# Earlier FFN weight and LayerNorm fetches, LayerNorms split from their transposes, weight loads on two queues and whole-row V copies in a memory-transformer kernel

## The chip, the cores and the metric

The kernel runs on one core of a Trainium2 chip. The metric is the device time of one execution in microseconds (us). Absolute times differ between chips: the kernel before took 1549 us (median) on the chip of the first comparison and 1564 to 1567 us on the chips of the three later calls. Kernels of different calls are compared by their ratio to the kernel before, which ran beside them on the same chip; kernels of one call also by their medians. A ratio is the mean time of one kernel's fast runs over the mean of the other's fast runs of the same rounds, so it is not quite the ratio of the medians quoted.

Stage boundaries are read from a profiled execution's timeline, in us from the start of the span. TensorE is called PE in the profile, VectorE DVE, ScalarE ACT, SyncE SP; SPq and ACTq are the instruction streams that issue DMAs.

## The reference, cut to what matters

```python
# x: 2048 x 640, bf16; 32 heads of 128; 8 memory rows; segments of 32 tokens
mem = mem0
for s in range(64):
    h = concat([mem, ln1(x)[32*s : 32*s+32]])        # 40 rows
    q, k, v = h @ Wq, h @ Wk, h @ Wv                 # 640 -> 32*128 each
    p = softmax(mask(q @ k.T * 128**-0.5))
    o = (p @ v) @ Wo                                 # 32*128 -> 640
    mem = o[:8]                                      # feeds the next segment
    attn[32*s : 32*s+32] = o[8:]
h  = x + attn
h2 = h + (relu(ln2(h) @ W_gate) * (ln2(h) @ W_up)) @ W_down      # 640 -> 1728 -> 640
```

The 64 segments form a chain through `mem`. The FFN at the end has no chain; it runs in 4 blocks of 512 rows.

## The kernel before

Operations are recorded in program order for each engine. A small dependency solver turns read and write keys (`r=`, `w=`) into semaphore waits. Each engine works strictly in its own order, and so does the SP queue that issues nearly all DMAs: a DMA that must wait holds up every later one. All DMAs carry the line of the helper, L298, so tile names tell them apart.

Names used below: a pass is the product with one weight matrix (the K pass with Wk, the Wo pass with Wo); KmT and Vr hold keys and values, oT the attention's output on its way into the Wo pass, xt the rows that a LayerNorm works on, hT the product of gate and up. LN1 and LN2 are the two LayerNorms; "row i" of LN2 is a block of 128 rows. "Segments 1 mod 4" are segments 1, 5, 9 and so on.

The FFN's tensors lie in the SBUF space of the attention weights: Wg and Wu in that of Wq, Wd in that of Wk, the rest in that of Wk and Wv. The parts that matter:

```python
# LN1: one piece, in every fourth segment, in PE order before KmT is copied
def ln1(b, n, bk):
    norm_rows(xt, ("xt",), n, xt, ("xt",))     # DVE statistics, ACT Ln and Exp, DVE scale
    transpose_rows(xt, ("xt",), n, bk)         # five PE transposes (L314)
    ...                                        # DVE copies to the operands of the passes

# LN2: one piece too
def ln2(i, bk):
    par, u, e = (i // 4) % 2, i % 4, i % 2     # two buffers xt2, at
    dma(x2, x_ap[128*i:128*i+128, :], r=[("Wdone",)], w=[xk])
    dma(a2, attn_d[...], r=attn_keys(i) + [("Wdone",)], w=[ak])
    add("dve", ... h = x2 + a2 ...)
    norm_rows(h, hk, 128, x2, xk)
    transpose_rows(x2, xk, 128, bk)
    copy_op("act", xn2T[par][...], ...)

# V rows for later segments, 8 pieces of 256 bytes in each row
dma(Vr[q][..., 0:Dh], Vp[par][..., 0:Dh], ...)

# start: all loads on SP
ld_init = ln1_load(-1)
for j in (1, 0, 2):
    for i in range(2):
        dma(W[:, j, :, 2048*i:2048*i+2048], ..., w=[("W", j, i)])
dma(Wo[:, :, :], ..., w=[("Wo",)])
ln1(-1, ld_init, XP0)
ln1(0, ln1_load(0), XP1)                       # second x block: behind all weights
... 64 segments ...
# after the last segment
dma(Wg, ..., w=[("W", 0, 0), ("W", 0, 1), ("Wg",)])
dma(Wu, ..., w=[("W", 0, 0), ("W", 0, 1), ("Wu",)])
dma(Wd[:, 0:FC-1, :], ..., w=[("W", 1, 0), ..., ("Wd", 0)])
dma(Wd[0:FR, FC-1, :], ..., w=[("W", 1, 0), ..., ("Wd", 1)])
... last attention outputs and their stores, ln2(0) to ln2(3) ...
for b in range(NBLK):
    for j in range(FC):
        gate_up(b, j)
        if b + 1 < NBLK and j in (2, 4, 6, 8):
            ln2(4*(b+1) + (2, 4, 6, 8).index(j), BT[j // 2 % 2])
    for u in range(4):
        down(b, u)
```

Wg and Wu both write the key `("W", 0, 0)`. To the solver that is a write after a write, so Wu waits until Wg has landed although they fill different bytes. The same holds for the two pieces of Wd.

The softmax here doesn't subtract the row's maximum and nothing guards it: scores larger than these inputs give would overflow.

## Time and profile before

Median 1548.69 us of 3 runs (1544.54 to 1549.66). The page of the kernel before: TensorE's busy time, its busy tenths and its granted clock in 40 equal slices of the span, and the DMA packets.

```profile
PE 1275.4 (82%) x36507; PEld 809.4 (52%) x36507; DVE 632.3 (41%) x1687; ACT 415.6 (27%) x736; POOL 4.1 (0%) x21
...
PE   0289898989898988988898889898989825878698
...
PEclk9999999999999999999999999999999967989899
...
DMA packets 86829, 58.02 MB, mean 37 GB/s; under 512 B 67376, under 2 KB 81392, under 8 KB 86512
```

PE is near full in the long middle. The holes are at the start, in slice 33 (segments to FFN) and, shallower, in the FFN. Why the start is empty is in the timeline of the SP queue (start, duration, what was issued):

```profile
8.89 1.15 SPq L298 DMA_DIRECT2D W<-in_A_Wk_dram  x2
...
11.38 19.17 SPq L298 DMA_DIRECT2D W<-in_A_Wv_dram  x2
30.59 6.20 SPq L298 DMA_DIRECT2D Wo<-in_A_Wo_dram  x1
36.91 20.98 SPq L298 DMA_DIRECT2D xt<-in_A_x_dram  x1
```

The second x block (`xt`) is issued after 21 MB of weights; its own issue blocks for 21 us, it lands at 65.4, and the first K pass starts at 68.3. The SP queue's own waits around the transition (total us, times, longest):

```profile
SPq L298 <- DMA Wd<-in_B_W_down_dram: 14.3, 1, 14.3
...
SPq L298 <- DMA Wg<-in_B_W_gate_dram: 9.0, 1, 9.0
```

These two are the shared keys at work: SP stood on Wu until Wg had landed, and on Wd's small last piece until Wd's main piece had landed. The longest of PE's waits between the last segment and the FFN (1240 to 1292) is for the first LN2 rows, whose loads stand behind all this on SP:

```profile
PE ps L314 <- DVE xt_0_98 L308: 26.1, 2, 23.2
```

Then PE's waits in the FFN:

```profile
PE ps L314 <- DVE xt_0_98 L308: 20.8, 6, 3.5
PE ps L314 <- DVE xt_1_99 L308: 20.8, 6, 3.5
```

Twelve times PE reached LN2's transposes (L314) and waited 3.5 us for DVE, in all 41.6 us. PE's waits in segments 2 to 62:

```profile
PE ps L564 <- issue: 31.8, 30, 1.6
PE ps L514 <- issue: 25.1, 32, 1.9
PE ps L314 <- DVE xt L308: 12.2, 14, 0.9
```

The third line is the same thing for LN1. "issue" means that PE waited for nothing that the profile shows. Laid beside the DMA records, every such gap ends 1.2 to 1.5 us (5th to 95th percentile) after a 16 KB packet of the instruction queue has finished, so I read them as PE running out of instructions. Counting gaps over 0.3 us, they are 83.7 us of segments 2 to 62. (The view counts from 0.15 us, so its lines add up to 1 to 3 us more. "Segments 2 to 62" are, here and below, the 60 segments from the end of segment 1's Wo pass to the end of segment 61's.)

### The profile page before, as it was taken

The numbers are of one execution on the slowest core, as the hardware profiler recorded it, in microseconds if no ns is written. First come the engines' busy times: TensorE is split into PE (matmuls) and PEld (weight loads), VectorE is DVE, ScalarE is ACT, GpSimd is POOL, SyncE is SP. The second block draws the span as 40 slices with busy tenths as digits, with TensorE's granted clock in tenths as the row PEclk, the third lists the DMA queues.
The fourth block names the chain that finished last, engine by engine and source line by source line (L and its number), as shares of the span: only waits on it lengthen the run. The fifth ranks groups of instructions, "written<-read, shape, count | busy, mean of one in ns | idle before, by whom it ended". The sixth has DMA issues, their size and how long they took to land.

```text
span 1554.2 us, 77215 instructions
## 1 busy us (share of the span) xinstructions
PE 1275.4 (82%) x36507; PEld 809.4 (52%) x36507; DVE 632.3 (41%) x1687; ACT 415.6 (27%) x736; POOL 4.1 (0%) x21
## 2 busy tenths in 40 slices
PE   0289898989898988988898889898989825878698
PEld 0156555656556555655665555565556622434254
DVE  1144444444444445444444444444444413232322
ACT  0032233333232333322232323323323202121211
POOL 1000000000000000000000000000000000000000
PEclk9999999999999999999999999999999967989899
DMA  7601110101000000100000001110000151011000
GB/s 294 253 14 19 21 21 17 22 15 24 17 21 17 20 17 21 21 21 17 21 21 17 20 17 22 19 22 17 18 17 16 25 183 51 9 43 34 17 18 18
DMA packets 86829, 58.02 MB, mean 37 GB/s; under 512 B 67376, under 2 KB 81392, under 8 KB 86512
## 3 DMA queue, kind: packets, MB, share of 16 engines
q1 hardware_dynamic: 86512, 53.09, 12.3%
q8 instruction: 285, 4.67, 1.3%
q14 instruction: 32, 0.26, 0.1%
HBM read 35.48 MB, written 5.24 MB: 26 GB/s over the span
## 4 chain that ended last, share of the span: by engine, by line
PE 74%; DVE 9%; issue 7%; DMA 4%; ACT 3%; SPq 3%; POOL 0%; DVEq 0%; POOLq 0%
PE ps L330 23%; PE ps L514 12%; PE ps L350 10%; PE ps L776 9%; PE ps L564 5%; PE ps L798 4%; PE ps L364 4%; SPq L298 3%; DVE tok_73 L337 2%; DMA xt<-in_A_x_dram 2%; DVE st L302 2%; PE ps L535 1%; PE ps L532 1%; PE ps L490 1%; PE ps L314 1%
## 5 line engine op out<-in xcount | busy, mean ns | idle before, releaser
L330 PE MATMUL ps<-W,act_r_67 128*32 128x512 bf16 x2680 | 154.9, 383 | 2.7 <-DVE rx L575 1.4
L330 PE MATMUL ps<-W,act_r_66 128*32 128x512 bf16 x2560 | 148.9, 384 | 2.4 <-issue 2.3
L335 ACT ACTIVATE tok_70<-ps 128x512 bf16<-128x512 f32 x65 | 38.8, 597 | 354.6 <-PE ps L330 354.6
L330 PEld LDWEIGHTS ps<-W,act_r_67 128*32 128x32 bf16 x2680 | 69.8, 97 | 74.2 <-DVE tok_71 L337 6.6
L514 PE MATMUL ps<-Wo,oT_88 128*32 128x160 bf16 x4224 | 88.2, 239 | 21.4 <-issue 16.1
L330 PEld LDWEIGHTS ps<-W,act_r_66 128*32 128x32 bf16 x2560 | 67.7, 97 | 71.5 <-issue 8.4
L337 DVE CAST tok_73<-ps 128x512 bf16<-128x512 f32 x92 | 63.6, 692 | 99.5 <-PE ps L330 97.4
L577 DVE TENSOR_TENSOR ox<-ps,rx 128x384 bf16<-128x384 f32 (+1 forms) x192 | 98.5, 513 | 6.6
L514 PE MATMUL ps<-Wo,oT_87 128*32 128x160 bf16 x4224 | 83.2, 236 | 13.2 <-DVE oT_87 L380 10.6
L514 PEld LDWEIGHTS ps<-Wo,oT_88 128*32 128x32 bf16 x4224 | 77.0, 99 | 30.7 <-issue 20.6
L335 ACT ACTIVATE tok_72<-ps 128x512 bf16<-128x512 f32 x92 | 54.9, 597 | 122.6 <-PE ps L330 122.6
L350 PE MATMUL ps<-W,act_r_67 128*32 128x512 bf16 x1360 | 85.6, 380 | 0.0
L514 PEld LDWEIGHTS ps<-Wo,oT_87 128*32 128x32 bf16 x4224 | 74.3, 98 | 21.2 <-DVE oT_87 L380 15.9
L350 PE MATMUL ps<-W,act_r_66 128*32 128x512 bf16 x1280 | 81.0, 380 | 0.0
L314 PE MATMUL ps<-ident,xt 128*128 128x128 bf16 (+1 forms) x85 | 7.8, 225 | 80.3 <-DVE xt L308 80.3
L337 DVE CAST tok_71<-ps 128x512 bf16<-128x512 f32 x65 | 45.0, 692 | 67.7 <-PE ps L330 67.7
L378 ACT ACTIVATE Kr<-ps 128x768 bf16<-128x768 bf16 (+3 forms) x74 | 52.4, 724 | 44.8 <-DVE KmT L380 43.4
L514 PE MATMUL ps<-Wo,oTe 128*32 128x160 bf16 x2048 | 45.4, 239 | 12.5 <-issue 12.5
L532 PE MATMUL ps<-Qr,Kr 128*32 128x32 bf16 x2048 | 46.6, 180 | 10.9 <-issue 10.9
L540 ACT ACTIVATE Px<-ps 128x512 bf16<-128x512 f32 x64 | 38.2, 597 | 62.1 <-PE ps L535 62.1
L378 ACT ACTIVATE Qr<-ps 128x768 bf16<-128x768 bf16 (+3 forms) x74 | 52.1, 723 | 1.5 <-PE ps L364 1.5
L564 PE MATMUL ps<-Vp_82,Px 8*32 8x129 bf16 x1024 | 37.6, 217 | 17.8 <-issue 17.8
(189 smaller groups left out, 2135.1 us busy)
## 6 DMA issues: line engine op xcount, KB each, us to landing
W<-in_A_Wk_dram SPq DMA_DIRECT2D x2, 2560.0 KB
W<-in_A_Wq_dram SPq DMA_DIRECT2D x2, 2560.0 KB
W<-in_A_Wv_dram SPq DMA_DIRECT2D x2, 2560.0 KB
Wo<-in_A_Wo_dram SPq DMA_DIRECT2D x1, 5120.0 KB
attn_d<-wtoke SPq DMA_DIRECT2D x256, 2.5 KB
xt<-in_A_x_dram SPq DMA_DIRECT2D x15, 160.0 KB
Wg<-in_B_W_gate_dram SPq DMA_DIRECT2D x1, 2160.0 KB
Wu<-in_B_W_up_dram SPq DMA_DIRECT2D x1, 2160.0 KB
```

Of the source, the lines that this page charges most:

```text
L330: ins = pe.matmul(bank(b)[32 * g:32 * g + 32, :], act[:, c, :], W[:, j, c, o:o + 512], start=(c == 0), stop=(c == DC - 1), skip_group_chec ...
L335: add("act", lambda a: a.activation(dst, bank(b), ACTF.Copy), r=[B(b)], w=[dkey])
L337: add("dve", lambda v: v.tensor_copy(dst, bank(b)), r=[B(b)], w=[dkey])
L350: ins = pe.matmul(bank(b)[32 * g:32 * g + 32, :], act[:, c, :], W[:, 2, c, o:o + 512], start=(c == 0), stop=(c == DC - 1), skip_group_chec ...
L364: ins = pe.matmul(bank_bf(b)[:, k * 128:(k + 1) * 128], t[:, (k % 4) * 128:(k % 4 + 1) * 128], ident[:, :], is_transpose=True)
L378: add("act", lambda a: a.activation(dst, src, ACTF.Copy), r=r, w=w)
L514: i = pe.matmul(bank(bk)[32 * gg:32 * gg + 32, 0:160], src[:, hb, :], w[:, gg], start=(hb == 0), stop=(hb == 31), skip_group_check=True)
L532: pe.matmul(bank(XS)[32 * g:32 * g + 32, k * 32:k * 32 + 32], Kr[:, 4 * k + g, p:p + 32], Qr[:, 4 * k + g, p:p + 32], start=True, stop=Tru ...
L564: i = pe.matmul(bank(XPB[k])[32 * g:32 * g + 32, o:o + 129], lh, rh, start=(a == 0), stop=(a == 1), skip_group_check=True, tile_position=( ...
L577: add("dve", lambda v, src=src, k0=k0, n=n: v.tensor_tensor(ox[:, k0:k0 + n, :], src[:, :, 0:128], ap(rx, k0, [[1, n], [0, 128]]), ALU.mul ...
L776: ins = pe.matmul(bank(bk)[0:nf, :], w[:, c, j * 128:j * 128 + nf], xn2T[par][:, c, :], start=(c == 0), stop=(c == DC - 1))
L798: i = pe.matmul(bank(bk)[:, 0:320], hT[par][0:nf, j, u * 128:(u + 1) * 128], Wd[0:nf, j, hf * 320:(hf + 1) * 320], start=(j == 0), stop=(j ...
```

## The change

Its intent: use the DMA system while PE is busy, and keep PE from standing in front of a DVE chain. It has six parts: (1) both first x blocks are loaded before the weights; (2) the weights are loaded on two queues, SP and ACT; (3) LN1's DVE part moves to the end of one segment, its transposes to the next; (4) Wg and Wu are fetched behind segment 62 and Wd behind segment 63, and LN2 rows 0 to 3 are processed within segment 63; the last attention outputs move into FFN block 0; (5) LN2's front and its transposes are two gate/up pairs apart; (6) V rows are copied whole, 2080 bytes in one piece.

```diff
-    dma(Vr[q][..., 0:Dh], Vp[par][..., 0:Dh], r=[("Vp", par)], ...)
+    dma(Vr[q][..., :], Vp[par][..., :], r=[("Vp", par), ("Vp1", par), ("Vr1", q)], ...)
...
-    ld_init = ln1_load(-1)
+    ln1_load(-1, xt, ("xt",))
+    ln1_load(0, x0, ("oTe", 0))
+    qs = ("sp", "act")
     for j in (1, 0, 2):
         for i in range(2):
-            dma(W[...], ..., w=[("W", j, i)])
-    dma(Wo[:, :, :], ..., w=[("Wo",)])
+            dma(W[...], ..., w=[("W", j, i)], eng=qs[i])
+    for i in range(2):
+        dma(Wo[:, 16*i:16*i+16, :], ..., w=[("Wo", i)], eng=qs[i])
...
-            if s % 4 == 1 and s // 4 + 1 in ln_loaded:
-                ln1(s // 4 + 1, ln_loaded[s // 4 + 1], XP1)
+            if s % 4 == 2 and ln:
+                ln1_back(nb, xt, ("xt",), XP1)
...
+        if s == NSEG - 2:
+            dma(Wg[:, :, :], ..., w=[("W", 0, 0), ("W", 0, 1), ("Wg",)])
+            dma(Wu[:, :, :], ..., w=[("W", 0, 0), ("W", 0, 1), ("Wu",)])
+        if last:
+            for i in range(2):
+                ln2_front(i)
+            dma(Wd[:, 0:FC - 1, :], ..., w=[("W", 1, 0), ("W", 1, 1), ("Wd", 0)])
+            dma(Wd[0:FR, FC - 1, :], ..., w=[("W", 1, 0), ("W", 1, 1), ("Wd", 1)])
...
         scores_x(s)
+        if last:
+            for i in range(2):
+                ln2_back(i, (T1, XP0)[i])
+                ln2_front(i + 2)
...
+        if s % 4 == 1 and ln:
+            ln1_front(nb, xt, ("xt",))
         if not last:
             trans_om(s)
...
             gate_up(b, j)
-            if b + 1 < NBLK and j in (2, 4, 6, 8):
-                ln2(4 * (b + 1) + (2, 4, 6, 8).index(j), BT[j // 2 % 2])
+            if b + 1 < NBLK and j % 3 == 1 and j < 12:
+                ln2_front(4 * (b + 1) + j // 3)
+            if b + 1 < NBLK and j % 3 == 0 and j:
+                ln2_back(4 * (b + 1) + j // 3 - 1, BT[j // 3 % 2])
+            if b == 0 and j < 4:
+                tail[j]()
```

Buffers move with it: `xt2`, `at`, the first block's rows and its transposed operand now lie in Wk's space, so that LN2 can start when the last K pass is done: an LN2 load now waits, through `("Wdone", 1)`, for the last pass that read Wk.

More of the change, by code (lines that the diff above doesn't have):

```diff
@@ L200, in build_kernel @@
     Wd = ffn.alloc("Wd", [128, FC, D], BF16)
+    xt2 = [ffn.alloc(f"xt2_{i}", [128, D], BF16) for i in range(2)]
+    at = [ffn.alloc(f"at{i}", [128, D], BF16) for i in range(2)]
+    h_rows = [[ffn.alloc(f"h0_{u}", [128, D], BF16) for u in range(4)]]
     g1 = [ffn.alloc(f"g1_{i}", [128, TB], BF16) for i in range(3)]
+    osb = [ffn.alloc(f"osb{i}", [128, D], BF16) for i in range(3)]
+    xn2T = [ffn.alloc("xn2T0", [128, DC, TB], BF16)]
+    assert ffn.off <= 2 * DC * HD * 2
+    ffn.off = 2 * DC * HD * 2
+    h_rows.append([ffn.alloc(f"h1_{u}", [128, D], BF16) for u in range(4)])
+    xn2T.append(ffn.alloc("xn2T1", [128, DC, TB], BF16))
     hT = [ffn.alloc(f"hT{i}", [128, FC, TB], BF16) for i in range(2)]
-    osb = [ffn.alloc(f"osb{i}", [128, D], BF16) for i in range(3)]
+    assert ffn.off <= ffn.size
     ident = ar.alloc("ident", [128, 128], BF16)
@@ L230, in build_kernel @@
     xt = ar.alloc("xt", [128, D], BF16)
-    xt2 = [ffn.alloc(f"xt2_{i}", [128, D], BF16) for i in range(2)]
-    at = [ffn.alloc(f"at{i}", [128, D], BF16) for i in range(2)]
     st = ar.alloc("st", [128, 2, 6], F32)
@@ L236, in build_kernel @@
     rs = ar.alloc("rs", [128, 1], F32)
-    h_rows, xn2T = [], []
-    for i in range(2):
-        h_rows.append([ffn.alloc(f"h{i}_{u}", [128, D], BF16) for u in range(4)])
-        xn2T.append(ffn.alloc(f"xn2T{i}", [128, DC, TB], BF16))
-    assert ffn.off <= ffn.size
     ps = es.enter_context(nc.psum_tensor("ps", [128, 4096], F32))
@@ L285, in build_kernel @@
             w=[("act", i, j, "m") for j in range(4)] + [("act", i, "x")])
-        add("pool", lambda p, i=i: p.memset(ap(Vp[i], Dh, [[VW, 8], [1, 1]]), 1.0), w=[("Vp1", i)])
+        add("pool", lambda p, i=i: p.memset(ap(Vp[i], Dh, [[VW, 8], [1, VW - Dh]]), 1.0), w=[("Vp1", i)])
         add("pool", lambda p, i=i: p.memset(wtok[i][:], 0.0), w=[("wtok", i)])
@@ L332, in f @@
             return ins
-        add("pe", f, r=list(akeys) + [("W", j, i)], w=[B(b)])
+        add("pe", f, r=list(akeys) + [("W", j, i)], w=[B(b), ("Wdone", j)])
         if eng == "act":
@@ L352, in f @@
             return ins
-        add("pe", f, r=list(akeys) + [("W", 2, i)], w=[B(b), ("Wdone",)])
+        add("pe", f, r=list(akeys) + [("W", 2, i)], w=[B(b), ("Wdone", 2)])
         src = bank(b).rearrange("p (k d) -> p k d", d=128)
@@ L409, in v_riders @@
                 a = 32 * g + M + done
-                dma(Vr[q][32 * g + o:32 * g + o + m, :, 0:Dh], Vp[par][a:a + m, :, 0:Dh], r=[("Vp", par)],
+                dma(Vr[q][32 * g + o:32 * g + o + m, :, :], Vp[par][a:a + m, :, :], r=[("Vp", par), ("Vp1", par), ("Vr1", q)],
                     w=[("Vr", q, g, o)])
@@ L415, in vr_keys, with ln1_front, ln1_load, ln1_back @@
         return [("Vr", q)] + [("Vr1", q)] + [("Vr", q, g, o) for g in range(4) for o in (0, 8, 16, 24)]
-    def ln1_load(b):
+    def ln1_front(b, buf, key):
         t0, n = (0, 64) if b < 0 else (64 + 128 * b, min(128, S - 64 - 128 * b))
-        dma(xt[0:n, :], x_ap[t0:t0 + n, :], w=[("xt",)])
-        return n
-    def ln1(b, n, bk):
-        norm_rows(xt, ("xt",), n, xt, ("xt",))
-        transpose_rows(xt, ("xt",), n, bk)
+        norm_rows(buf, key, n, buf, key)
+    def ln1_load(b, buf, key):
+        t0, n = (0, 64) if b < 0 else (64 + 128 * b, min(128, S - 64 - 128 * b))
+        dma(buf[0:n, :], x_ap[t0:t0 + n, :], w=[key])
+    def ln1_back(b, buf, key, bk):
+        n = 64 if b < 0 else min(128, S - 64 - 128 * b)
+        transpose_rows(buf, key, n, bk)
         src = bank_bf(bk)[:, 0:DC * 128].rearrange("p (c t) -> p c t", t=128)
@@ L511, in f @@
                 for hb in range(16 * hf, 16 * hf + 16):
+                    assert head(hb // 4, hb % 4) // 16 == hf
                     w = Wo[:, head(hb // 4, hb % 4), :].rearrange("p (c g j) -> p g c j", g=4, j=32)
@@ L516, in f @@
                 return i
-            add("pe", f, r=list(keys) + [("Wo",)], w=[B(bk)])
+            add("pe", f, r=list(keys) + [("Wo", hf)], w=[B(bk)])
         if 1 in halves:
@@ L593, in attn_keys, with ln2_front @@
         return ks
-    def ln2(i, bk):
+    def ln2_front(i):
         par, u, e = (i // 4) % 2, i % 4, i % 2
         x2, xk, a2, ak = xt2[e], ("xt2", e), at[e], ("at", e)
-        dma(x2[:, :], x_ap[128 * i:128 * i + 128, :], r=[("Wdone",)], w=[xk])
-        dma(a2[:, :], attn_d[128 * i:128 * i + 128, :, :].rearrange("t g f -> t (g f)"), r=attn_keys(i) + [("Wdone",)],
+        dma(x2[:, :], x_ap[128 * i:128 * i + 128, :], r=[("Wdone", 1)], w=[xk])
+        dma(a2[:, :], attn_d[128 * i:128 * i + 128, :, :].rearrange("t g f -> t (g f)"), r=attn_keys(i) + [("Wdone", 1)],
             w=[ak])
@@ L607, in ln2, with ln2_back @@
         norm_rows(h, hk, 128, x2, xk)
-        transpose_rows(x2, xk, 128, bk)
+    def ln2_back(i, bk):
+        par, u, e = (i // 4) % 2, i % 4, i % 2
+        transpose_rows(xt2[e], ("xt2", e), 128, bk)
         copy_op("act", xn2T[par][:, :, 128 * u:128 * u + 128],
@@ L615, in build_kernel @@
             mem0_ap.rearrange("t (c g j) -> g t c j", g=4, j=32)[g], r=[("wtok", 1)], w=[("wtok0", g)])
-    ld_init = ln1_load(-1)
+    x0 = oTe[:].rearrange("p h t -> p (h t)")[:, 0:D]
+    ln1_load(-1, xt, ("xt",))
+    ln1_load(0, x0, ("oTe", 0))
     srcs = (A_Wq, A_Wk, A_Wv)
+    qs = ("sp", "act")
     for j in (1, 0, 2):
@@ L621, in build_kernel @@
                 srcs[j].rearrange("(c p) h e -> p c (h e)", c=DC, p=128)[:, :, 2048 * i:2048 * i + 2048],
-                w=[("W", j, i)])
-    dma(Wo[:, :, :], A_Wo.rearrange("h e d -> e h d"), w=[("Wo",)])
-    ln1(-1, ld_init, XP0)
-    ln1(0, ln1_load(0), XP1)
+                w=[("W", j, i)], eng=qs[i])
+    for i in range(2):
+        dma(Wo[:, 16 * i:16 * i + 16, :], A_Wo.rearrange("h e d -> e h d")[:, 16 * i:16 * i + 16, :], w=[("Wo", i)],
+            eng=qs[i])
+    ln1_front(-1, xt, ("xt",))
+    ln1_back(-1, xt, ("xt",), XP0)
+    ln1_front(0, x0, ("oTe", 0))
+    ln1_back(0, x0, ("oTe", 0), XP1)
     add("dve", lambda v: v.transpose(TBf[:].rearrange("p c t -> p (c t)"), wtok[1][:].rearrange("p c t -> p (c t)")),
@@ L654, in build_kernel @@
     v_riders(0, 64, RID)
-    ln_loaded = {}
     def extra_units(s):
@@ L685, in woe_store @@
                     r=[("wtoke",)], w=[("attn", t0, g)])
+    fullr = (FC - 1) * 128
     for s in range(NSEG):
@@ L689, in build_kernel @@
         par = s % 2
-        if s % 4 == 0 and 64 + 128 * (s // 4 + 1) < S:
-            ln_loaded[s // 4 + 1] = ln1_load(s // 4 + 1)
+        nb = s // 4 + 1
+        ln = 64 + 128 * nb < S
+        if s % 4 == 0 and ln:
+            ln1_load(nb, xt, ("xt",))
         if s > 0:
@@ L713, in build_kernel @@
                 v_riders(par, t0, nr)
+        if s == NSEG - 2:
+            dma(Wg[:, :, :], B_W_gate.rearrange("(c p) f -> p c f", p=128), w=[("W", 0, 0), ("W", 0, 1), ("Wg",)])
+            dma(Wu[:, :, :], B_W_up.rearrange("(c p) f -> p c f", p=128), w=[("W", 0, 0), ("W", 0, 1), ("Wu",)])
+        if last:
+            for i in range(2):
+                ln2_front(i)
+            dma(Wd[:, 0:FC - 1, :], B_W_down[0:fullr, :].rearrange("(j p) d -> p j d", p=128),
+                w=[("W", 1, 0), ("W", 1, 1), ("Wd", 0)])
+            dma(Wd[0:FR, FC - 1, :], B_W_down[fullr:F, :], w=[("W", 1, 0), ("W", 1, 1), ("Wd", 1)])
         units, fin = extra_units(s)
@@ L740, in build_kernel, with wo_last, woe_last @@
             fin()
-    dma(Wg[:, :, :], B_W_gate.rearrange("(c p) f -> p c f", p=128), w=[("W", 0, 0), ("W", 0, 1), ("Wg",)])
-    dma(Wu[:, :, :], B_W_up.rearrange("(c p) f -> p c f", p=128), w=[("W", 0, 0), ("W", 0, 1), ("Wu",)])
-    fullr = (FC - 1) * 128
-    dma(Wd[:, 0:FC - 1, :], B_W_down[0:fullr, :].rearrange("(j p) d -> p j d", p=128),
-        w=[("W", 1, 0), ("W", 1, 1), ("W", 2, 0), ("W", 2, 1), ("Wd", 0)])
-    dma(Wd[0:FR, FC - 1, :], B_W_down[fullr:F, :],
-        w=[("W", 1, 0), ("W", 1, 1), ("W", 2, 0), ("W", 2, 1), ("Wd", 1)])
-    trans_ox(NSEG - 1, T1)
-    for k, s in enumerate((NSEG - 2, NSEG - 1)):
-        par = s % 2
-        wo_pass(oT[par], [("oT", par, "m"), ("oT", par, "x")], BM, wtok[par], ("wtok", par), "dve")
-        store_attn(wtok[par], ("wtok", par), M, 32 * s, RID)
-    wo_pass(oTe, oTe_keys, XP0, wtoke, ("wtoke",), "act")
-    woe_store(NSEG // 4 - 1)
-    BG, BU, BD, BT = (0, 1), (2, 3), (4, 5), (6, 7)
-    for u in range(4):
-        ln2(u, BT[u % 2])
+    BG, BU, BD, BT = (0, 1), (2, 3), (4, 5), (6, 7)
+    for i in (2, 3):
+        ln2_back(i, BT[i % 2])
+    tail = [lambda: trans_ox(NSEG - 1, BT[0])]
+    for s in (NSEG - 2, NSEG - 1):
+        par = s % 2
+        def wo_last(s=s, par=par):
+            wo_pass(oT[par], [("oT", par, "m"), ("oT", par, "x")], BT[par], wtok[par], ("wtok", par), "dve")
+            store_attn(wtok[par], ("wtok", par), M, 32 * s, RID)
+        tail.append(wo_last)
+    def woe_last():
+        wo_pass(oTe, oTe_keys, BT[0], wtoke, ("wtoke",), "act")
+        woe_store(NSEG // 4 - 1)
+    tail.append(woe_last)
     n_g = [0]
```

## The prediction

> **What bounds it now.** TensorE is busy 82% of the 1554 us profiled span. Stages, from the timeline and windows view:
> - 0-68.4 us: TensorE idle, all weights load at about 410 GB/s. The second x block (xt) is queued behind all weights and lands at 65.4; only then does the first K pass run. First Wo pass: 97.3.
> - 100-1215: 64 recurrent segments of 17-21 us.
> - 1240-1291: Wg (9.4 us from issue to landing; Wu is issued only when Wg has landed), Wu+Wd (15.3), 24 attention stores, four LN2 chains. First gate matmul at 1291.3.
> - FFN blocks: 72.2, 68.9, 70.5, then 51 us for the one without LN2. LN2 transposes wait 41.6 us for DVE (waits view, 12 times 3.5 us); 3.4 us half-clock windows follow those stalls.
>
> **Startup.** Each pass can now begin when its weights land. Two queues add no bandwidth: the Trainium skill ("DMA: Bandwidth & Descriptors", "Issuing engines are not separate DMA queues") says they share the same 16 engines; here one queue alone made 410 GB/s. ACT starts at about 2 us, SP at about 9.5 us, then they share. My estimate: Wk's SP half at 25, Wq's at 38, Wv's at 50 us; then V passes plus the 10.3 us that today separate the first V pass from the first Wo pass: about 60 instead of 97. ACT may block on its fourth issue, as SP does today on its fifth (12.9 us); slack hides most. Gain 37 (28-42).
>
> **Segments.** LN1: TensorE waits 13.1 us (15 times) for xt. After: 2.3 us of DVE work and two ACT operations stand before the oT copy that feeds the Wo pass. DVE idles 2.5 us there, but Ln waits behind the wtoke copy, so the oT copy slips 1.2 us. Net 0 to +8 us; I take +4. V copies: 256-byte packets become 2080-byte ones; no TensorE wait names Vr: 0. The "issue" gaps (84 us here, each ending 1.4 us after a 16 KB instruction fetch) stay.
>
> **Transition.** Wg issues after segment 62's V copies (1225 on the old axis) and lands at 1234.5. Wu still waits for Wg because both write the same key, and SP is in order, so the first LN2 loads follow at 1236.5, behind Wu in the ring, landing about 1245. Wd's short tail piece waits for Wd's main piece (about 1252), and the LN2 loads 2 and 3 queue behind it; their chains end about 1261. First gate matmul: 1262 instead of 1291. TensorE idles about 15 us there. Gain 29, less 8 us of tail work moved into block 0.
>
> **FFN.** Front and back are two gate/up pairs apart (4.3 us); a front needs about 3.3 us on DVE after the hT product, so stalls vanish. Blocks with LN2: 51 us (30.4+17 matmuls, 2.9 transposes), block 0 with tail 59. Gain 211.6-161 = 51 (tail included).
>
> **Sum.** 1549-37-29-51+4 = 1436 us; range 1410-1464. Faster by over 2%: 0.97; within 2%: 0.025; slower: 0.005.
>
> **Signs.** First K pass near 25 us and first Wo pass near 60; LN2 transposes waiting under 8 us in the FFN; segment length unchanged within 0.3 us; first gate matmul 20-30 us after the last segment's passes, with DMA waits just before; DMA packets down by about 42,000.
>
> **What would break it.** LN2 loads landing before Wu (transition gain up to 45); ACT blocked long at startup; instruction fetches slowed by weight traffic; LN1's front costing over 1 us per fourth segment; DVE unable to keep up with hT plus fronts.

## The result and the profile after

The changed kernel took 1439.53 us (median of 4, 1432.36 to 1441.94), the kernel before 1549.18 us (median of 4, 1544.54 to 1551.91). Ratio 0.9287, 95% interval 0.9247 to 0.9328: faster, and 3.5 us above the predicted time. Stages from the two timelines:

| stage (us) | before | changed | difference | predicted |
|---|---|---|---|---|
| start to first K pass | 68.3 | 30.6 | | |
| first K pass to first Wo pass | 29.0 | 30.6 | -36.1 for both | -37 |
| first Wo pass to the end of the last V pass | 1137.8 | 1133.3 | -4.5 | +4 |
| last V pass to first gate matmul | 56.2 | 28.4 | -27.8 | -29 |
| FFN block 0 (with the tail since the change) | 72.1 | 65.7 | -6.4 | -13 |
| FFN blocks 1 and 2 | 68.9, 70.5 | 49.3, 49.3 | -40.8 | -37 |
| FFN block 3 | 51.4 | 51.5 | +0.1 | 0 |
| span | 1554.2 | 1438.6 | -115.6 | |

The profiled execution of the kernel before was a long one (1555.9 us against a median of 1549), so the spans differ by 6 us more than the medians. The -4.5 of the table's third line is inside the noise: in a second look at the changed kernel, on another chip, that stage took 1141.8 us.

The page of the changed kernel, the same lines as before:

```profile
PE 1254.5 (87%) x36507; PEld 803.2 (56%) x36507; DVE 631.0 (44%) x1687; ACT 411.3 (29%) x736; POOL 4.1 (0%) x21
...
PE   1989898989898989898989898989898984899998
...
PEclk9999999999999999999999999999999997899999
...
DMA packets 44733, 58.21 MB, mean 40 GB/s; under 512 B 19264, under 2 KB 33280, under 8 KB 44416
```

The holes shrank, and half of the packets are gone. Timelines of the SP and the ACT queue at the start:

```profile
9.46 0.55 SPq L298 DMA_DIRECT2D W<-in_A_Wk_dram  x1
...
11.29 19.23 SPq L298 DMA_DIRECT2D Wo<-in_A_Wo_dram  x1
```

```profile
0.83 0.41 ACTq L298 DMA_DIRECT2D W<-in_A_Wk_dram  x1
...
2.42 6.89 ACTq L298 DMA_DIRECT2D Wo<-in_A_Wo_dram  x1
```

ACT issues its first weight load 8.6 us ahead of SP. From the DMA records: SP's first weight packet starts only at 15.6 us, because memory rows and x rows stand before it on that queue; between 10 and 20 us SP's queue moves 103 GB/s and ACT's 286; between 20 and 30 us each queue moves about 205 GB/s; between 30 and 45 us, when SP carries packets of 4096 bytes and ACT packets of 1280, they move 297 and 99. The sum stays near 400, as on one queue before. SP's own waits in the transition:

```profile
SPq L298 <- DMA Wd<-in_B_W_down_dram: 11.2, 1, 11.2
SPq L298 <- DMA Wg<-in_B_W_gate_dram: 8.8, 1, 8.8
```

Both waits on shared keys are still there. PE's longest wait between the last segment and the FFN is shorter, but of the same kind:

```profile
PE ps L314 <- DVE xt_0_54 L308: 10.4, 1, 10.4
```

Of PE's waits for LN2 in the FFN (41.6 us) one is left, in block 0:

```profile
PE ps L314 <- DVE xt_1_55 L308: 4.8, 1, 4.8
```

And PE's waits in segments 2 to 62:

```profile
PE ps L568 <- issue: 27.7, 30, 1.6
PE ps L518 <- DVE oT_102 L380: 20.0, 26, 1.8
PE ps L518 <- issue: 19.2, 19, 2.0
```

LN1's wait for xt has gone from this list. A wait of the Wo pass for the oT copy has come: 29.3 us over both oT buffers (14.0 before), some 1.1 us in each of 14 segments. That was predicted (1.2). What was not: the gaps called issue fell from 83.7 to 74.1 us.

The windows view gives the granted clock by stage (length, busy times, then PEclk, DMA share and GB/s). Here are FFN blocks 1 of both, before and then changed:

```profile
1363.40:1432.30 68.90, 54.27 (x274) 25.97 (x273) 21.32 (x42) 13.16 (x26) 0.00 (x0) 0.93 0.09 29
```

```profile
1288.60:1337.90 49.30, 48.53 (x274) 25.15 (x274) 21.33 (x42) 12.45 (x26) 0.00 (x0) 1.00 0.13 41
```

The same work on DVE and ACT now fits under 48.5 us of matmuls, and the clock no longer drops. The Trainium skill ("TensorE: Matmul & The Clock Gate", "What's actually happening") says that PE goes to half its clock after an idle window of about 3.4 us. The trace agrees in form: after LN2's waits the clock records of the kernel before show half-clock stretches of 3.4 to 6.8 us, and in blocks 1 and 2 of the changed kernel none. But the 3.4 us before need not be idle: before the half-clock stretch at 195.3 us of the changed kernel, in the segments, PE was busy for 2.2 of them, and its longest wait there was 1.2 us.

### The profile page after: what moved, and what is told of

Same layout as the page of the kernel before. It is cut to its first block, busy times and chain, and to the rows that moved or that the text cites. A ratio compares the mean times of both kernels' runs of the same rounds, so it can differ in the third digit from the quotient of the medians.

```text
span 1438.6 us, 77225 instructions
## 1 busy us (share of the span) xinstructions
PE 1254.5 (87%) x36507; PEld 803.2 (56%) x36507; DVE 631.0 (44%) x1687; ACT 411.3 (29%) x736; POOL 4.1 (0%) x21
## 4 chain that ended last, share of the span: by engine, by line
PE 78%; DVE 7%; issue 6%; DMA 4%; ACT 3%; SPq 1%; POOL 0%; DVEq 0%; POOLq 0%
PE ps L330 23%; PE ps L518 13%; PE ps L350 11%; PE ps L804 8%; PE ps L364 6%; PE ps L568 5%; PE ps L826 5%; DMA W<-in_A_Wv_dram 3%; DVE tok_87 L337 1%; PE ps L539 1%; PE ps L493 1%; PE ps L536 1%; SPq L298 1%; PE ps L472 1%; ACT Kr L378 1%
## 5 line engine op out<-in xcount | busy, mean ns | idle before, releaser
L330 PEld LDWEIGHTS ps<-W,act_r_81 128*32 128x32 bf16 x2680 | 69.8, 98 | 84.4 <-DMA W<-in_A_Wk_dram 8.8
L518 PE MATMUL ps<-Wo,oT_102 128*32 128x160 bf16 x4224 | 85.2, 238 | 27.8 <-DVE oT_102 L380 22.6
L330 PEld LDWEIGHTS ps<-W,act_r_80 128*32 128x32 bf16 x2560 | 67.7, 98 | 71.5 <-issue 8.9
L518 PEld LDWEIGHTS ps<-Wo,oT_102 128*32 128x32 bf16 x4224 | 76.3, 99 | 35.8 <-DVE oT_102 L380 27.6
L518 PE MATMUL ps<-Wo,oT_101 128*32 128x160 bf16 x4224 | 83.9, 236 | 13.4 <-DVE oT_101 L380 10.2
L518 PEld LDWEIGHTS ps<-Wo,oT_101 128*32 128x32 bf16 x4224 | 74.6, 98 | 22.0 <-DVE oT_101 L380 15.7
L350 PEld LDWEIGHTS ps<-W,act_r_81 128*32 128x32 bf16 x1360 | 34.4, 96 | 34.8 <-issue 2.0
L518 PE MATMUL ps<-Wo,oTe 128*32 128x160 bf16 x2048 | 43.2, 233 | 11.8 <-issue 11.8
L539 PE MATMUL ps<-Qr,KmT 128*32 128x32 bf16 x2048 | 45.3, 180 | 4.7 <-issue 4.6
```

What stands on the lines that cost most here:

```text
L330: ins = pe.matmul(bank(b)[32 * g:32 * g + 32, :], act[:, c, :], W[:, j, c, o:o + 512], start=(c == 0), stop=(c == DC - 1), skip_group_chec ...
L350: ins = pe.matmul(bank(b)[32 * g:32 * g + 32, :], act[:, c, :], W[:, 2, c, o:o + 512], start=(c == 0), stop=(c == DC - 1), skip_group_chec ...
L518: i = pe.matmul(bank(bk)[32 * gg:32 * gg + 32, 0:160], src[:, hb, :], w[:, gg], start=(hb == 0), stop=(hb == 31), skip_group_check=True)
L539: i = pe.matmul(bank(XS)[32 * g:32 * g + 32, 256 + k * 32:256 + k * 32 + 32], KmT[:, 4 * k + g, :], Qr[:, 4 * k + g, p:p + 32], start=True ...
```

## The experiments

My theory at this point: the startup gain is the early x rows plus ACT's earlier start, not bandwidth; the transition is held by serialized loads; block 0 is held by stores that stand before a load; the FFN gain is the split of LN2; LN1's split and the V copies give nothing. All outputs are right. The gaps called issue, and lengths of segments "net" of them, are for segments 2 to 62.

First a measure of the noise: the changed kernel was profiled twice. Segments 2 to 62 took 1085.3 us in the first look and 1095.4 in the second, with 11.4 and 27.3 us of half clock in that stretch. So ten microseconds of total segment length between two profiles prove nothing by themselves. Where the code is the same, stage lengths elsewhere repeat within about 2 us, and the gaps lie between 72.8 and 82.8 us in all ten profiles that have LN1 as in the changed kernel.

### One queue for the weights

```diff
-    qs = ("sp", "act")
+    qs = ("sp", "sp")
```

> The changed kernel with all weight loads on the SP queue, x rows still first. My theory: both queues together move no more than one (about 410 GB/s), so what the second queue buys is only that it starts at 1 us instead of 9.5, about 8 us of transfer; against that, one queue delivers Wk first. First K pass near 18-20 us (30.6 in the changed kernel), last half of Wo near 65 us (about 60), so the first Wo pass starts at 58-62 and stalls in its middle; total 2 to 6 us slower than the changed kernel (ratio to before about 0.932). Rival: two queues carry more than one, or hide more; then the loading stage grows by 10 us or more.

Ratio 0.9266 (0.9218 to 0.9313), median 1451.4, which is 5.2 us above the next kernel. First K pass at 19.3 us, first Wo pass at 62.5, with pieces of waiting for Wk, Wq, Wv and Wo between them; segment 2 began 4.9 us later than in the changed kernel. The first Wo pass is 0.5 us outside of the expected range, and the ratio, expected near 0.932, lies between the two of the changed kernel (0.9287 and 0.9254); but the loading stage did not grow by the rival's 10 us. So two queues bought about 5 us by starting earlier. Counted to the start of segment 2 (120.3 us before, 91.2 here, 86.4 changed), about 29 of the 34 us belong, by difference, to the early x rows.

### The old V copies

```diff
-    dma(Vr[q][..., :, :], Vp[par][..., :, :], ...)
+    dma(Vr[q][..., :, 0:Dh], Vp[par][..., :, 0:Dh], ...)
```

> The changed kernel with the old V copies of 256-byte pieces; packets back up by about 42,000. My prediction was that the whole-row copies give nothing: the total stays within 3 us of the changed kernel, segments keep their length. Rival, from the comparison of the two traces: fewer packets let the instruction fetches arrive sooner (mean fetch 1057 to 1013 ns, TensorE gaps of kind issue 83.7 to 74.1 us over segments 2 to 62); then the gaps come back to about 84 us and the total is 8 to 10 us longer. A third: the gaps shift only because the order of instructions changed; then they stay near 74 us here.

Ratio 0.9238 (0.9196 to 0.9280), so not slower than the changed kernel (0.9287, and 0.9254 in its second comparison). 86,845 packets, issue gaps 74.8 us. The mean 16 KB instruction fetch of PE (the expectation's 1057 and 1013 count smaller fetches too) took 1114 ns over segments 2 to 62 against 1073 in the changed kernel's first look, but 1119 in its second. So neither the fetch time nor the gaps follow the packets, and the gaps stayed where the third reading has them. Whole-row copies halve the packet count and give nothing that these runs resolve.

### LN1 in one piece

```diff
-            if s % 4 == 2 and ln:
+            if s % 4 == 1 and ln:
+                ln1_front(nb, xt, ("xt",))
                 ln1_back(nb, xt, ("xt",), XP1)
...
-        if s % 4 == 1 and ln:
-            ln1_front(nb, xt, ("xt",))
```

> The changed kernel with the first LayerNorm in one piece again, in every fourth segment before KmT. My theory: the split only swapped one wait for another, so undoing it changes little: TensorE's wait for xt returns to about 13 us, its wait for oT falls from 33 to about 15 us, segments 1 mod 4 about +0.8 us, 2 mod 4 about -0.6 us without their issue gaps; total within 5 us of the changed kernel. Rival: the split is worth the whole 13 us wait; then 10 to 15 us slower.

Ratio 0.9316 (0.9278 to 0.9354); median 1459.4, which is 13.1 us above the kernel with old V copies. The waits moved as the theory said (xt 12.2 us, oT 13.5), but the total did not stay within 5 us. Net of issue gaps the segments took 1014.8 us against 1011.2; the issue gaps took 89.8 against 74.1. The theory that the split only swaps one wait for another had failed, and the extra time was in a place that I had called unaffected.

### LN1's front after the oT copy

If the split gains because the moved wait costs little where it now is, then removing that wait too should gain little.

```diff
-        if s % 4 == 1 and ln:
-            ln1_front(nb, xt, ("xt",))
         if not last:
             trans_om(s)
+        if s % 4 == 1 and ln:
+            ln1_front(nb, xt, ("xt",))
```

> The changed kernel with LN1's front emitted after the oT copy instead of before it. It tells what the moved wait costs. In the changed kernel TensorE waits about 30 us for oT over segments 2 to 62 (14 before), but has fewer gaps of kind issue than with LN1 joined (74-80 against 84-90). Theory A: the moved wait falls where TensorE would have starved for instructions anyway, so it is half free; then here the oT wait falls to about 14 us, the segments net of issue gaps fall by 13-17 us, but the issue gaps rise to 82-90, total 4 to 10 us faster. Theory B: issue gaps are chance of the order of instructions; then they stay near 75 and the total is 13 to 17 us faster.

The oT wait fell to 13.8 us and net of issue gaps the segments fell to 1001.7 us, by 9.5. The issue gaps rose to 97.8 us, by 23.7. (Against the changed kernel's second look, which like this one had much half clock, 27.3 and 23.9 us, it is 14.1 and 18.2.) The edit moves work of DVE and ACT only: PE's matmuls and their order are the same, so a changed order is not what brought the gaps. Ratio 0.9257 (0.9196 to 0.9318): not faster than the changed kernel. Theory A has the direction right and the size too small: the gaps took back the whole gain. Segment 33 shows how, in PE's waits. Changed kernel, then LN1 later, then LN1 joined (from its second run, below):

```profile
PE ps L518 <- DVE oT_102 L380: 1.7, 1, 1.7
PE ps L536 <- issue: 1.1, 1, 1.1
PE ps L568 <- issue: 0.9, 1, 0.9
```

```profile
PE ps L518 <- issue: 1.4, 1, 1.4
PE ps L536 <- issue: 1.4, 1, 1.4
PE ps L568 <- issue: 1.2, 1, 1.2
```

```profile
PE ps L568 <- issue: 1.5, 1, 1.5
PE ps L518 <- issue: 1.2, 1, 1.2
PE ps L536 <- issue: 0.9, 1, 0.9
PE ps L314 <- DVE xt L308: 0.9, 1, 0.9
PE ps L493 <- DVE Pbd L478: 0.3, 1, 0.3
```

Before the Wo pass (L518) PE stands still in all three: for the oT copy in the first, for instructions in the other two. Where it waits for data, the next instructions arrive meanwhile, and the gap of kind issue at that line is gone. In the joined form PE waits for xt at a place where the other two show no gap, and starves later all the same.

### Changed and joined again, on one chip

```diff
(no edit; the changed kernel)
```

> The changed kernel itself again, unaltered, as the measure for the others of this call. Expected: ratio to before 0.925 to 0.930, issue gaps in segments 2 to 62 between 72 and 83 us, oT wait near 30 us.

```diff
(the edit of "LN1 in one piece")
```

> The changed kernel with LN1 joined, again, now beside the changed kernel on one chip. The first look at it was 13 us slower than the run with old V copies, of which its profile shows 3.6 us net of issue gaps and 15 us in issue gaps. If the split really saves TensorE time by moving a wait onto instruction starvation, this is 8 to 15 us slower than the changed kernel beside it and its issue gaps are 84 us or more; if the first look was chance, the difference is under 5 us.

Changed: median 1448.9 of 6 (1444.3 to 1453.2), ratio 0.9254 (0.9221 to 0.9287), issue gaps 79.6 us. Joined: median 1458.8 of 6 (1452.4 to 1460.7), ratio 0.9309 (0.9276 to 0.9341), issue gaps 90.6 us. The joined form is 9.9 us slower by the medians, and its issue gaps are 11.0 us larger. The segments net of the gaps are not longer (1012.9 against 1015.8). The three profiles with LN1 in one piece, the kernel before among them, have 83.7, 89.8 and 90.6 us of gaps, all above the ten with LN1 as in the changed kernel. So the split of LN1 was worth 10 to 13 us by the medians (9 to 12 by the means), and it is seen in the gaps.

### LN2 in one piece in the FFN

```diff
-            if b + 1 < NBLK and j % 3 == 1 and j < 12:
-                ln2_front(4 * (b + 1) + j // 3)
-            if b + 1 < NBLK and j % 3 == 0 and j:
-                ln2_back(4 * (b + 1) + j // 3 - 1, BT[j // 3 % 2])
+            if b + 1 < NBLK and j in (2, 4, 6, 8):
+                ln2_front(4 * (b + 1) + j // 2 - 1)
+                ln2_back(4 * (b + 1) + j // 2 - 1, BT[j // 2 % 2])
```

> The changed kernel with LN2's front and transposes back to back in the FFN blocks, after pairs 2, 4, 6 and 8. My theory: the split gives the whole FFN gain; blocks 1 and 2 go back from 49.3 to 69-71 us each, block 0 from 65.7 to 75-80, half-clock windows of 3.4 us return; total 50 to 57 us slower, about 1491 us, ratio to before about 0.963. Rival: part of the gain comes from loads that are now issued earlier or from the full clock alone; then blocks 1 and 2 come out at 60 or less.

Blocks 89.3, 68.9, 70.5 and 51.2 us; median 1512.1, ratio 0.9646 (0.9597 to 0.9696). Blocks 1 and 2 are back where they were before the change, so the split is the whole gain there, and the rival is out. The total is 66 us above the kernel with old V copies, not 50 to 57, because block 0 came out longer than expected. PE's waits for LN2 rows in the FFN:

```profile
PE ps L314 <- DVE xt L308: 49.9, 12, 10.0
```

The longest, in block 0, is now 10.0 us, and the loads for that row stand on SP behind the last 16 stores of the tail; I take that as the reason but tested it only with the split LN2 (below).

### Own keys for Wg, Wu and Wd

```diff
-  dma(Wg[...], ..., w=[("W", 0, 0), ("W", 0, 1), ("Wg",)])
-  dma(Wu[...], ..., w=[("W", 0, 0), ("W", 0, 1), ("Wu",)])
+  dma(Wg[...], ..., r=[("Wdone", 0)], w=[("Wg",)])
+  dma(Wu[...], ..., r=[("Wdone", 0)], w=[("Wu",)])
   (the two pieces of Wd likewise, with ("Wdone", 1))
```

> The changed kernel, but Wg, Wu and the two pieces of Wd no longer write a common key: each waits only for the last pass that read the old weights, not for the load before it. My theory: in the transition the in-order SP queue stood 9 us on Wu (for Wg to land) and 11.6 us on Wd's tail piece (for Wd's main piece to land), with the LN2 loads behind both. Expected: Wu issued right after Wg, the first LN2 load lands 4 to 6 us earlier, loads 2 and 3 about 9 us earlier; time from the last V pass to the first gate matmul 28.4 to 17-21 us; total 8 to 11 us faster. Rival: the bytes themselves, not the waits, hold the LN2 loads back; then it stays above 26 us.

Last V pass to first gate matmul: 22.1 us instead of 28.4, so 6.3 us less and 1 us outside of the range. The waits on Wg and Wd are gone from the SP queue. What it stands on now is PE's transposes, which must free one of the two buffers before row 2 can be loaded (L121 is the solver's wait):

```profile
SPq L121 <- PE ps L314: 5.7, 2, 3.9
```

The shared keys were about 6 of the 28 us; the two buffers look like the next limit, which was not tested alone. The total (two runs, ratio 0.9204, 0.9128 to 0.9279) is too coarse to add to this.

### Loads before the tail's stores

`ln2_front` was cut in two; the loads come one slot earlier than the arithmetic.

```diff
             if b + 1 < NBLK and j % 3 == 1 and j < 12:
-                ln2_front(4 * (b + 1) + j // 3)
+                u = j // 3
+                for v in ((0, 1), (2,), (3,), ())[u]:
+                    ln2_load(4 * (b + 1) + v)
+                ln2_front(4 * (b + 1) + u)
```

> The changed kernel with the loads of LN2 rows issued one slot before they are used in the FFN, so that the second row's loads stand before the 24 attention stores of the tail on the SP queue and not behind the last 16 (5.3 us). My theory: block 0 lost 5 us of wait for row 5 (and half-clock time after it) to that; block 0 falls from 65.7 to 58-61 us, blocks 1 and 2 stay at 49.3; total 5 to 8 us faster. Rival: block 0 is long because of the tail's own TensorE work and DVE copies; then it stays above 63.

Block 0 took 60.0 us instead of 65.7, blocks 1 and 2 stayed at 49.3, and PE waited for no LN2 row in the FFN. That is the missing part of block 0: the 16 stores of the last memory rows take SP 5.3 us to issue, and the loads for row 5 stood behind them. (Two runs, ratio 0.9220, 0.9125 to 0.9315.)

### Weights before the memory rows

```diff
-    (the four memory-row loads first on SP)
     ln1_load(-1, xt, ("xt",))
     ln1_load(0, x0, ("oTe", 0))
     dma(W[:, 1, ...])                          # Wk
+    (the four memory-row loads here)
     dma(W[:, 0, ...]) ...
```

> The changed kernel with the SP queue issuing the x rows and Wk's first half before the four memory-row loads, which wait for a memset until 5.2 us. My theory: what holds the first K pass at 30.6 us is that SP's half of Wk starts at 9.5 us and then shares the engines with ACT's transfers, which ran ahead. Expected: K's first pass at 17-20 us, the first Wo pass at 54-57 instead of 61.2 (bounded by Wv and Wo landing), total 4 to 7 us faster. Rival: the total of bytes sets it, then the first Wo pass stays at 60 or later although K starts early.

The first K pass moved from 30.6 to 21.9 us, but the first Wo pass only from 61.2 to 59.8. My numbers (17 to 20, and 54 to 57) missed. PE finished the K passes and then waited for Wq (total us, times, longest; the window is the first 62 us):

```profile
PE ps L330 <- DMA W<-in_A_Wq_dram: 6.6, 1, 6.6
```

So an early start of K is not worth much: the order in which the bytes arrive only decides where in the prologue PE waits. There was a second cost: ACT stood 12.9 us in the issue of its half of Wo, and the first LayerNorm's Ln and Exp, which ACT runs, came only at 15.4 us. (Two runs, ratio 0.9244, 0.9162 to 0.9326.)

### The parts together

```diff
+    xt2, at: four buffers, two in what Wq's space has left beside Wg and Wu
+    segment 62: ln2_load(0), ln2_load(1) on SP; Wg, Wu on ACT, own keys
+    segment 63: after the K pass ln2_load(2), ln2_load(3), then Wd, own keys;
+        ln2_front(0) before V, (1) after KmT, (2) and (3) around the Wo pass;
+        transposes in free PSUM banks; the tail's first Wo pass before the FFN
+    ln2_load(4) to (7) before the FFN; later ones at j == 0
     LN1 as in the changed kernel
```

> The changed kernel improved where the experiments point: own keys for Wg, Wu and Wd; four buffers for LN2 rows instead of two, two of them in the old Wq space so that they load behind segment 62, ahead of all FFN weights; Wg and Wu on the ACT queue; LN2 fronts spread through the last segment; one tail Wo pass moved into the wait before the FFN; loads of FFN block 0 issued before the tail's stores. My theory (the transition was held by serialized loads and by LN2 buffers, block 0 by the stores): last V pass to first gate matmul 28.4 to 9-13 us, block 0 from 65.7 to 56-59 us; total 22 to 28 us faster than the changed kernel of the same call. Rival: DVE's four fronts of 2.7 us and the weight traffic hold it; then the gap stays above 18 us.

Median 1422.2 of 6 (1416.3 to 1429.8), ratio 0.9087 (0.9052 to 0.9122). On the same chip the changed kernel took 1448.9 and the kernel before 1563.9: it beats both, the changed kernel by 26.7 us, as expected. Last V pass to first gate matmul took 17.7 us, not the expected 9 to 13 and only just under the rival's 18, and block 0 took 54.6, better than 56 to 59. In the 17.7 us PE now does one of the tail's Wo passes (3.9 us at a low clock), and it starves once for longer than in any other look:

```profile
PE ps L570 <- issue: 3.7, 1, 3.7
```

The two stages together are 21.8 us shorter than in the changed kernel's first profile, and 23.9 us shorter than in its second, on this chip (29.0 and 67.2 us). What each part of the edit gave was not separated, and the rest of the 26.7 us is not explained by these edits. The profiled execution had only 4.4 us of half clock in segments 2 to 62, and I leave that open.

```diff
(the parts together, with the SP order of "Weights before the memory rows")
```

> The combined kernel with the SP order of the earlier run (x rows and Wk's half before the memory rows). There it brought the first K pass forward by 8.7 us but the first Wo pass by only 1.4. Expected: 0 to 3 us faster than the combined kernel, not resolved by the time; first Wo pass near 60 us.

Median 1423.1, ratio 0.9091 (0.9059 to 0.9124): the same time as without it. First Wo pass at 60.1 us.

## Why the prediction was right or wrong

The time was right (1436 predicted, 1439.5 measured), but the sum hides misses that cancel, and that they do is luck.

- **Startup, -37: measured -36.1.** Right in size, and "two queues add no bandwidth" held. The Trainium skill ("DMA: Bandwidth & Descriptors", "Issuing engines are not separate DMA queues") says so, and here one queue moved about 410 GB/s and two moved 205 each. "Wk's SP half at 25" was wrong: the first K pass started at 30.6, because SP's first weight packet started only at 15.6 us and its queue then got half of the 410 GB/s. The passes that followed found their weights nearly all landed (0.5 us of wait for Wv), so the late K pass and 18.7 us of K and Q passes, and not the landing of Wv as predicted, set the time. It did little harm: with K at 21.9 us the landing set it, and the first Wo pass came only 1.4 us earlier.
- **LN1, +4: wrong in sign.** The failed step is "Net 0 to +8 us; I take +4", with its tail, "The 'issue' gaps ... stay". The oT copy did slip as computed, by about 1.1 us. But I added that wait to the time as if PE would otherwise have worked through it. The runs show that PE would have starved for instructions at that place. The wait covers the starvation, and undoing the split costs 9.9 us on one chip, seen as 11.0 us more of issue gaps. It is this pair that shows the sign, and not the -4.5 of the table. The sign "segment length unchanged within 0.3 us" failed too: with all gaps included, segments 1 mod 4 went from 20.9 to 19.6 us and segments 2 mod 4 from 16.9 to 17.7.
- **V copies, 0: right.** Also the packets: 42,096 fewer.
- **Transition, -29: measured -27.8.** Right, and for the reason given: SP still waited 8.8 us on Wg and 11.2 on Wd. The arithmetic of rows 0 and 2 on DVE waited 7.3 and 4.8 us for their loads to land. Own keys bring the stage down by 6.3 us; the combined kernel, with four buffers and earlier loads among its edits, brings it to 17.7. The first gate matmul came 28.4 us after the last passes, within the "20-30".
- **FFN, -51: measured -47.1.** Two sizes were off in opposite ways. Blocks 1 and 2 took 49.3 us each, not 51: that no stall was left had been predicted, but the four transposes were counted at 2.9 us and take 1.8 (0.44 each), and the sum of 50.3 was rounded up. Block 0 took 65.7 us, not 59: the prediction gave the tail 8 us of PE time and forgot its 24 stores on the in-order SP queue. The last 16 of them held the loads for row 5; without that, block 0 takes 60.0.

## What to carry to other kernels

An in-order issue queue makes every key a possible barrier: give loads that fill different bytes different keys, and place loads that feed the next step ahead of stores that nobody waits for. Put a chain on another engine a few steps ahead of the PE instruction that needs it; here that removed 37 of 42 us of waits in the FFN, all of them once the loads stood before the stores, and the half-clock time after them. Before adding up PE waits, look where PE is short of instructions: a wait placed there can cost nothing, and removing it can gain nothing.

## What the Trainium skill lacked or had wrong

- "Runtime: NRT & Kernel Launch", "Instruction fetch mechanics" says that crossing a 16 KiB block is mostly hidden, because the sequencer dispatches more slowly than the fetch fills. Here PE stood 73 to 98 us of about 1090 (segments 2 to 62) in gaps that each end 1.2 to 1.6 us after a 16 KB fetch has finished (5th to 95th percentile in every trace). Most come where PE runs through many small matmuls: 128 weight loads and 128 matmuls in 2.4 us in a Wo pass. The page does not say that a data wait at such a place can be free.
- "DMA: Bandwidth & Descriptors", "Issuing engines are not separate DMA queues" says that initiating from several engines saves only issue time that is usually small. Here that time was not small, because an issue can block: SP stood 12.9 us in its fifth weight load before the change (the first Wv half, 11.4 to 24.3) and 21.0 us in the issue of the small x block behind Wo; ACT stood 6.9 us and, in one experiment, 12.9 us in its fourth. In that experiment the first LayerNorm's Ln, which ACT runs, came at 15.4 us, though its input was ready at 7.9. No page that I read gives the depth at which an issue blocks.
- The same page, "Queues, rings and completion order", says that an engine alternates between queues by packets. The trace agrees and adds the consequence: with packets of 4096 bytes on one queue and of 1280 on the other, the queues moved 297 and 99 GB/s, a ratio of 3.0 against 3.2 for the sizes; the profile counts 1088 and 1096 packets in these 15 us, so nearly one for one.
- "TensorE: Matmul & The Clock Gate", "What's actually happening" gives half the clock to an idle window of about 3.4 us, and speaks of chance from run to run only at a kernel's start. Here half clock also came after 3.4 us in which PE was busy for 2.2 (at 195.3 us), and the same kernel had 11.4 and 27.3 us of it in the same 60 segments, far from its start. The two looks were 10 us apart in length; that the one causes the other was not tested.
